# One attention and two mixing layers on one core: three more heads transposed by TensorE, and part of VectorE's, ScalarE's and GpSimd's work handed round

## The chip, the core and the metric

The kernel runs on one core of a Trainium2 chip. The metric is device time in microseconds (us) from one launch to its end. The core has five engines with a queue each: TensorE (PE, whose weight loads are a row of their own, PEld), VectorE (DVE), ScalarE (ACT), GpSimd (POOL) and SyncE (SP, which here only issues DMAs). An engine runs its instructions strictly in the order in which they were put; an instruction that waits holds up all that stand behind it.

## The reference

All of it is computed in float32 accuracy, from float32 activations and float64 weights:

```
B, H, S, D = 4, 8, 576, 64                      # 32 heads in all
scores = q @ k.T / 8 + cum[:, None] - cum[None, :], causal   # cum = cumsum(log f)
attn   = exp(scores - max) / sum ;  x = attn @ v             # x: (4, 576, 512)
h = relu(x.T @ w_tok1) @ w_tok2 ;   u = x + h.T              # token mix, 576 -> 256 -> 576
x = u + relu(u @ w_ch1) @ w_ch2                              # channel mix, 512 -> 1536 -> 512
h = relu(x @ w_in) ; c = conv3(h) along S                    # gated layer, 512 -> 1024
out = (h * sigmoid(c)) @ w_out                               # 1024 -> 512
```

## The kernel before, in words

**Products.** Nearly all matmuls are done as three float16 products of a high and a low half (`mm3`, lines 279 to 284: high by high at L282, high by low at L283 and low by high at L284; `w` and `z` in the names are PSUM banks). Each operand is scaled by a power of two found at run time, then split: the high half is the scaled value cast to float16, the low half is what the cast lost.

**Attention.** 32 heads, taken in pairs and in groups of four (group g is heads 4g to 4g+3). For a pair, `score` (PE, L1009 and L1013) makes the scores in blocks, `smax` (DVE, L1027) adds the mask and takes the maximum, and `sexp` (ACT, L1033) gives the unnormalised probabilities `t` (buffers t_193 to t_196 in turn: head 8 is t_193, head 11 is t_196). P has to be transposed before P times V. There are two ways. The heads in the list `BY_PE` (0 to 7 and 31) are *turned by TensorE*: 13 transposes of 128x128 float32 a head (`ptr`, L1066), then copies out of PSUM; for heads 8 and up these are a high half by ACT (L1084) and a low half by DVE (L1087). All other heads are split first, the high half `ph` by POOL (`hi_part`, L1042, a piece of 1024 and one of 640 columns), the low half `pl` by DVE (`lo_part`, L1048), and each half is turned by a DMA transpose that SP issues. P times V is float32 for heads 0 to 7 (L1098) and float16 triples for the others (L1103 to L1105, 45 matmuls a head). `norm` and `xout` (DVE) divide and write `xf`; `x_hi`, `x_lo` and `x_scale` make the halves `xh` and `xl` and a scaled copy. `x_hi` is on POOL for heads below `XHP`, else on ACT; `x_lo` (L277) and `x_scale` (L1143) are on POOL.

**V.** For each group, `v_tasks` makes high and low halves of V on POOL (L274 and L921) in two buffers in turn, vp_205 for group 2 and vp_206 for group 3.

**Token mix**, after each group (`group`): T1 (30 matmuls, from `xh` and `xl` of the four heads), T2 (24 matmuls with transposes of `xf`), then squares for the size of u. After the second group of a batch, `u_span` on PE spreads the size (`um`, L262), DVE makes the scale `su` of it (L251 to L257), and ACT and DVE make the halves `uh` and `ul` (L610 and L613).

**Channel mix.** The 1536 columns are cut into 12 blocks of 128, the blocks into parts of 5, 4 and 3. Part 0 (blocks 0 to 4) is done while attention still runs, as filler with a rank far behind (`LATE`): `m1` (u by w_ch1), `rh` on ACT and `rl` on DVE for relu and split, `m2` (by w_ch2), result to memory. Parts 1 and 2 follow attention. Then comes the gated layer in eight chunks.

**Weights.** `weight_set` prepares five blocks: load (SP), float64 to float32 (ACT L319, DVE L323 and L324), squares (ACT L520) for the size, spread over the partitions by PE (`stat_c`, L262), a power of two by DVE (`pw_c`, L251 to L257), then scaling and halves. By the argument `on_pool` these are three POOL instructions a block (L555 scaled, L274 high, L277 low), or ACT for the high (L570) and DVE for the low half (L574). `ONP` says which, for c1 (w_ch1) and c2 (w_ch2) of part 0: before, c1 is on POOL and c2 is not. In the listings of the order, w_113 to w_117 are c1's blocks and w_118 to w_122 are c2's; a block's halves go to the buffer one place lower, c1's first one to w_123.

**What sets the order.** The class `Order` plans all of it when the program is built: each piece is a task with engine, estimated cost, rank, what it reads and writes, and its turn in the PSUM banks (`z` 2, `w` 4). It goes through the tasks in order of the time at which they could begin by those estimates, lower rank first where two could begin together, and so fixes each engine's instruction order. At run time only that order remains. The ranks come from constants: `TOKR` and `TOKP` (token weights), `SETR` and the paces behind it (channel weights), `AVAIL` and `LATER` (channel mix).

Of the kernel before, what the change touches and what calls it, by code (L numbers as in the profile page):

```python
# [13 lines left out]
AF = mybir.ActivationFunctionType  # L14
ALU = mybir.AluOpType
# [128 lines left out]
def fox_moe_kernel(  # L144
# [14 lines left out]
    nc = tc.nc  # L159
    NH, D, QKW = qk.shape  # L160
    B, S, H, _ = v.shape
# [12 lines left out]
    HG = 4  # L174
# [16 lines left out]
    PSC = 2.0 ** 15  # L191
# [10 lines left out]
    MM = 0.1226  # L202

    FULL = 2 * HG
    TURNED = 2 * HG
    LAST = 1
    BY_PE = [n < TURNED or n >= NH - LAST for n in range(NH)]

    TOKR, TOKP = 10.0, 5.0
    VRANK = 4.0  # L210
    XHP = 8
    ONP, TONP = (2, 0), (1, 1)
    SETR = ((-20.0, 0.0),)
    LATER = (-30.0, 10.0, 30.0)
    PER = 7.0

    const = ctx.enter_context(tc.tile_pool(name="const", bufs=1))
# [82 lines left out]
    T = todo.add  # L300
# [466 lines left out]
    with tc.manual_schedule():  # L767
# [72 lines left out]
        for a, n in ((DEC12 - 64, 64), (0, 64), (DEC12, WD[1]), (DEC12 + WD[1], WD[2])):  # L840
# [4 lines left out]
            out=mask[:, 512:640], in_=mask[:, 512:640], pattern=[[-1, 128]],  # L845
            compare_op=ALU.is_ge, fill=-8e9, base=0, channel_multiplier=1)

        TB = 4
# [123 lines left out]
        h_t = {}  # L972
# [65 lines left out]
        def hi_part(n, part):  # L1038
            if n not in h_t:
                h_t[n] = ap2.tile([128, PW], F16, tag="ph", name="ph", bufs=2)  # L1040
            sl = PARTS[part]
            nc.gpsimd.tensor_scalar(h_t[n][:, sl], t_t[n % TB][:, sl], PSC, 0.0, ALU.mult, ALU.add)  # L1042

        def lo_part(n, part):
            if n not in l_t:
# [102 lines left out]
        SEG = ((4, 3), (2, 1, 0))  # L1148

        def pair(p):  # L1150
            t0 = 2 * p * PER
            kq = ("qk", p % QKB)
            A2, A3, A1 = ["a2"], ["a2", "a3"], ["a1"]
            if p:
                T("SP", 0.4, t0 - 9, load_qk, p, writes=[kq], moved=2.6, pools=A2)
            for blocks in SETS:
                second = blocks == JOINED[1]
                kz = [turn("z") for _ in range(2 if blocks == (4,) else 1)] if not second else [kj]
                if blocks == JOINED[0]:
                    kj = turn("z")  # L1160
                T("PE", PE_S[blocks], -1e6 if second else t0 + 1, score, p, blocks, reads=[kq], writes=[*kz, ("scores",)],
                  pools=A2 + A1, ring=kz + [kj] if blocks == JOINED[0] else kz)
                for x, i in ((x, i) for x in range(2) for i in blocks[::-1]):
                    n = 2 * p + x
                    kt = ("t", n % TB)
                    rank = t0 + x * PER
                    T("DVE", DVE_S[i], rank + 2, smax, n, i, reads=[kz[x % len(kz)]], writes=[(*kt, i), ("m", n % 3, i)],
                      pools=A2 + A1, ring=[kz[x % len(kz)]])
                    T("ACT", ACT_E[i], rank + 3, sexp, n, i, reads=[("m", n % 3, i)], writes=[(*kt, i)], pools=A2)
            for n in (2 * p, 2 * p + 1):  # L1170
                rank = n * PER
                kt = ("t", n % TB)
                g = n // HG
                if BY_PE[n]:
                    for a, blks in enumerate(QUADS):
                        kw = turn("w")
                        kx = ("q", n % 2, a)
                        T("PE", 0.11 * len(blks), rank + 4, ptr, n, a, reads=[(*kt, i) for i in SEG[a // 2]],
                          writes=[kw, ("pth", n % 2, a), ("ptl", n % 2, a)], pools=A2 + A1, ring=[kw])
                        if n < FULL:  # L1180
                            T("DVE" if a == 2 else "ACT", 0.14 + 0.115 * len(blks), rank + 4, ptr_copy, n, a, reads=[kw],
                              writes=[("pth", n % 2, a), ("ptl", n % 2, a)], pools=A2 + ["a3"], ring=[kw])
                            continue
                        T("ACT", 0.15 + 0.12 * len(blks), rank + 4, ptr_hi, n, a, reads=[kw], writes=[("pth", n % 2, a)],
                          pools=A2 + ["a3"], ring=[kw])
                        T("DVE", 0.12 + 0.17 * len(blks), rank + 4, ptr_lo, n, a, reads=[kw, ("pth", n % 2, a)],
                          writes=[("ptl", n % 2, a)], pools=A2 + ["a3"], ring=[kw])
                else:
                    for q in range(2):
                        T("POOL", (1.22, 1.05)[q], rank + 4, hi_part, n, q, reads=[(*kt, i) for i in SEG[q]],  # L1190
                          writes=[("ph", n % 2, q)], pools=A2)
                    T("SP", 1.5, rank + 5, transp, n, 0, reads=[("ph", n % 2, 0), ("ph", n % 2, 1)],
                      writes=[("pth", n % 2, a) for a in range(len(QUADS))], moved=2.5, pools=A3)
                    for q in range(2):
                        T("DVE", (1.35, 0.9)[q], rank + 4, lo_part, n, q,
                          reads=[(*kt, i) for i in SEG[q]] + [("ph", n % 2, q)], writes=[("pl", n % 2, q)], pools=A2)
                    T("SP", 1.5, rank + 5, transp, n, 1, reads=[("pl", n % 2, 0), ("pl", n % 2, 1)],
                      writes=[("ptl", n % 2, a) for a in range(len(QUADS))], moved=2.5, pools=A3)
                vk = [("vp", g % 2, q, x) for q in range(3) for x in "hl"]
                kw = turn("w")  # L1200
                kp = [(x, n % 2, a) for x in ("pth", "ptl") for a in range(len(QUADS))]
                for i in ORDER:
                    T("PE", (0.22 if n < FULL else 0.1) * len(PVB[i]), rank + 6, pv, n, i, reads=[*kp, *vk], writes=[kw, ("xf", g % 2, n % HG)],
                      pools=["a3"], ring=[kw])
                T("DVE", 0.5, rank + 6, norm, n, reads=[kw, ("vsc", g % 3)], writes=[("rs", n % 2)], pools=A1, ring=[kw])
                T("DVE", 0.46, rank + 6, xout, n, reads=[kw, ("rs", n % 2)], writes=[("xf", g % 2, n % HG)], pools=A1, ring=[kw])
                T("POOL" if n < XHP else "ACT", 0.47, rank + 6, x_hi, n, reads=[("xf", g % 2, n % HG)], writes=[("xh", n % HG)], pools=A1)
                T("POOL", 1.05, rank + 6, x_lo, n, reads=[("xf", g % 2, n % HG), ("xh", n % HG)],
                  writes=[("xl", n % HG)], pools=A1)
                T("POOL", 0.6, rank + 7, x_scale, n, reads=[("tac",)], writes=[("xf", g % 2, n % HG)], pools=A1)  # L1210
# [146 lines left out]
        W1K = [("tokw", "t1", k) for k in range(3)]  # L1357
        W2K = [("tokw", "t2", k) for k in range(2 * KT)]
        v_tasks(0, -8)
        AVAIL = [(H * (b + 1) - 1) * PER + 30 for b in range(B)]  # L1360
        LATE = 1000.0
        tpw = []
        for name, ws, slots, q, factor in (("t1", tok_w[:3], (9, 10, 11), TOKR, 4.0),
# [13 lines left out]
        for x in range(EARLY):  # L1377
            n = PARTS_M[x]
            for y, (name, w, factor) in enumerate((("ch1", w_ch1, 4.0), ("ch2", w_ch2, 2.0 ** 13))):
# [1 line left out]
                q = t0 + SETR[x][y]  # L1381
                pw = weight_set(f"c{y + 1}{x}", [(name, m, (col_block if y == 0 else row_block)(w, m)) for m in ms],
                                list(range(at, at + n)), at - 1 if at else 2 * M1,
                                [q + 4.0 * k for k in range(n)], [q + 4.0 * n + 2.5 * k for k in range(n)], factor, ONP[y])
                if y == 0:
                    pws.append([pw])
                else:
# [247 lines left out]
```

## Time and profile before

| | |
|---|---|
| three runs | 715.43, 719.58 and 719.69 us, median 719.58 |
| the profiled execution | 718.21 us, of which the span of the profile is 716.4 |
| PE busy | 698.0 us, 97% of the span, 6417 matmuls |
| PE weight loads | 562.5 us, 79% |
| DVE, ACT, POOL busy | 499.3 (70%), 429.6 (60%), 267.9 us (37%) |
| chain that ended last | PE 82%, POOL 6%, DVE 5%, ACT 3%, DMA 2% |

Busy time is the union of an engine's instructions in the span; matmuls overlap in their pipeline, so the time from one matmul's start to the next one's is shorter than the duration given for one. PEclk is the granted TensorE clock as a share of full speed. A row of the timeline gives the start, the duration, the engine, the line and the instruction, with its tile names and how many follow in a row; a bracket behind it says how long the engine was idle before it and what ended that.

### The profile page before, as it was taken

To read this page: it belongs to the slowest core of one execution; us is meant where nothing else is said; L and a number is where in the kernel's file an instruction comes from. 1 tells how busy PE (TensorE), PEld (TensorE's weight loads), DVE (VectorE), ACT (ScalarE), POOL (GpSimd) and SP (SyncE) were. 2 spreads that over 40 slices of the span, in tenths; PEclk is the share of its full clock that TensorE was granted. 3 is DMA by queue.
4 is the path that set the end of the run, shared out by engine and by line. 5 is a ranking of instruction groups with operands and counts; after the bars stand their busy time and mean duration, and the time that the engine had idled before them with its cause. 6 is when DMAs were issued, how large, how long until landed. Compare 5 with 4: busy or idle time off the path is not lost.

```text
span 716.4 us, 16405 instructions
## 1 busy us (share of the span) xinstructions
PE 698.0 (97%) x6417; PEld 562.5 (79%) x6417; DVE 499.3 (70%) x1259; ACT 429.6 (60%) x943; POOL 267.9 (37%) x344
## 2 busy tenths in 40 slices
PE   7999989799999999999999999999999999999998
PEld 6888777587778787887888778778878778778786
DVE  6778989888876788437566856545778866875570
ACT  6777896476855684546664543312177766776671
POOL 2145899548672857230000211102023322323240
PEclk9999999899999999999999999999999999999999
DMA  9435988899994997875454855345211121100101
GB/s 220 131 94 175 218 263 192 153 231 258 213 234 104 239 163 180 206 266 153 153 186 123 275 186 173 100 134 153 66 48 58 51 59 35 54 23 26 35 18 50
DMA packets 152974, 101.99 MB, mean 142 GB/s; under 512 B 89984, under 2 KB 145024, under 8 KB 152896
## 3 DMA queue, kind: packets, MB, share of 16 engines
q1 hardware_dynamic: 152800, 100.79, 53.8%
q8 instruction: 50, 0.82, 0.5%
q14 instruction: 28, 0.23, 0.1%
q10 hardware_dynamic: 96, 0.15, 0.1%
HBM read 57.73 MB, written 23.59 MB: 114 GB/s over the span
## 4 chain that ended last, share of the span: by engine, by line
PE 82%; POOL 6%; DVE 5%; ACT 3%; DMA 2%; issue 1%; DVEq 0%; POOLq 0%; ACTq 0%
PE w L282 14%; PE w L284 14%; PE w L283 14%; PE z L283 8%; PE z L282 8%; PE z L284 8%; PE z L1009 5%; PE w L1098 2%; POOL vp L921 2%; PE w L1250 1%; DMA wraw<-in_moe_w_ch_dram 1%; PE w L1104 1%; PE z L1013 1%; PE w L1105 1%; PE w L1103 1%
## 5 line engine op out<-in xcount | busy, mean ns | idle before, releaser
L284 PEld LDWEIGHTS <-w 128*128 128x128 f16 x1280 | 125.4, 98 | 36.2 <-DVE w L574 4.0
L282 PEld LDWEIGHTS <-w 128*128 128x128 f16 x1280 | 125.0, 98 | 34.6 <-issue 2.7
L283 PEld LDWEIGHTS <-w 128*128 128x128 f16 x1280 | 125.1, 98 | 33.6 <-issue 2.7
L282 PE MATMUL w<-uh,w 128*128 128x288 f16 x416 | 119.0, 286 | 0.4 <-DVE r L666 0.4
L284 PE MATMUL w<-uh,w 128*128 128x288 f16 x416 | 119.0, 286 | 0.2 <-POOL w L277 0.2
L283 PE MATMUL w<-ul,w 128*128 128x288 f16 x416 | 119.0, 286 | 0.0
L277 POOL TENSOR_TENSOR g<-sg,g 128x286 f16<-128x286 f32 (+1 forms) x64 | 55.1, 867 | 150.2 <-ACT g L271 148.5
L1535 DVE SCALAR_TENSOR_TENSOR cv<-hp,cw,cv 128x286 f32<-128x286 f32 (+1 forms) x128 | 75.1, 593 | 38.3 <-ACT cv L1529 36.0
L662 ACT ACTIVATE r<-w 128x288 f16<-128x288 f32 x96 | 39.1, 408 | 90.7 <-PE w L284 90.6
L1033 ACT ACTIVATE t<-t,m 128x576 f32<-128x576 f32 (+4 forms) x160 | 81.3, 552 | 17.4 <-DVE m L1027 17.2
L739 POOL TENSOR_TENSOR p<-p,u 128x288 f32<-128x288 f32 x32 | 26.6, 861 | 151.2 <-DVE wraw L323 78.1
L1027 DVE CUSTOM_DVE_ANT_0 t<-z,mask 128x576 f32<-128x576 f32 (+4 forms) x160 | 69.9, 478 | 12.7 <-PE z L1013 12.6
L666 DVE SCALAR_TENSOR_TENSOR r<-w,r 128x288 f16<-128x288 f32 x96 | 43.3, 452 | 47.4 <-ACT r L662 46.8
L283 PE MATMUL z<-g,w 128*128 128x286 f16 (+1 forms) x256 | 73.3, 286 | 0.0
L282 PE MATMUL z<-g,w 128*128 128x286 f16 (+1 forms) x256 | 73.0, 285 | 0.0
L284 PE MATMUL z<-g,w 128*128 128x286 f16 (+1 forms) x256 | 72.9, 285 | 0.0
L284 PE MATMUL w<-vh,w 128*128 128x288 f16 x224 | 64.1, 286 | 0.0
L282 PE MATMUL w<-vh,w 128*128 128x288 f16 x224 | 64.1, 286 | 0.0
L282 PE MATMUL z<-r,w 128*128 128x288 f16 x224 | 64.1, 286 | 0.0
L283 PE MATMUL w<-vl,w 128*128 128x288 f16 x224 | 64.1, 286 | 0.0
L283 PE MATMUL z<-r,w 128*128 128x288 f16 x224 | 64.1, 286 | 0.0
L284 PE MATMUL z<-r,w 128*128 128x288 f16 x224 | 64.1, 286 | 0.0
(207 smaller groups left out, 1713.1 us busy)
## 6 DMA issues: line engine op xcount, KB each, us to landing
wraw<-in_moe_w_ch_dram SPq DMA_DIRECT2D x24, 512.0 KB, 4.7
qk<-in_qk_dram SPq DMA_DIRECT2D x16, 608.0 KB, 5.2
u_d<-us SPq DMA_DIRECT2D x8, 576.0 KB, 3.9
p_d<-res SPq DMA_DIRECT2D x32, 144.0 KB, 3.6
p<-p_d SPq DMA_DIRECT2D x8, 576.0 KB, 5.2
u<-u_d SPq DMA_DIRECT2D x8, 576.0 KB, 5.2
x_d<-p SPq DMA_DIRECT2D x8, 576.0 KB, 3.2
u<-x_d SPq DMA_DIRECT2D x8, 576.0 KB, 3.9
```

Of the source, the lines that this page charges most:

```text
L277: nc.gpsimd.tensor_tensor(o, a, b, ALU.subtract)
L282: nc.tensor.matmul(ps, wh, xh, start=(first and i == 0), stop=False)
L283: nc.tensor.matmul(ps, wh, xl, start=False, stop=False)
L284: nc.tensor.matmul(ps, wl, xh, start=False, stop=(last and i == n - 1))
L662: nc.scalar.activation(out=t[:, 0, :], in_=box["z", m], func=AF.Relu)
L666: nc.vector.scalar_tensor_tensor(t[:, 1, :], box["z", m], 0.0, f32(t[:, 0, :]), ALU.max, ALU.subtract)
L739: nc.gpsimd.tensor_tensor(box["p"][:, d], box["p"][:, d], box["u"][:, d], ALU.add)
L921: nc.gpsimd.tensor_tensor(low, t, hi, ALU.subtract)
L1009: nc.tensor.matmul(out_[x], t[r, Q0[i]:Q0[i] + 128], t[r, k0:k0 + n], start=first, stop=False)
L1027: nc.vector.tensor_tensor_reduce(to, z_t.pop((n, i)), mk, -0.125, 3e38, ALU.add, ALU.min, m_t[n][0:rows, i:i + 1])
L1033: nc.scalar.activation(out=tt[0:rows, o:o + w], in_=tt[0:rows, o:o + w], func=AF.Exp, bias=m_t[n][0:rows, i:i + 1], scale=-1.0)
L1535: nc.vector.scalar_tensor_tensor(cv, hp_t[m][:, s0 + t:s1 + t], cw[:, t, m:m + 1], cv, ALU.mult, ALU.add)
```

## The change

Heads 8, 9 and 30 join those that PE turns (`TURNED` 8 to 10, `LAST` 1 to 2). Of the heads that stay with the DMA transpose, two of three (n modulo 3 below 2: 13 heads) get their high half from ACT and one of three (7 heads: 11, 14, 17, 20, 23, 26, 29) from POOL as before. `x_hi` of heads 8 to 11 goes from ACT to POOL (`XHP` 8 to 12). The second set of channel weights, c2 of part 0, goes to POOL (`ONP` (2, 0) to (2, 2)). The remaining lines change ranks and the planner's estimates.

```diff
-    TURNED = 2 * HG
-    LAST = 1
+    TURNED = 10
+    LAST = 2
     BY_PE = [n < TURNED or n >= NH - LAST for n in range(NH)]
-    TOKR, TOKP = 10.0, 5.0
-    VRANK = 4.0
-    XHP = 8
-    ONP, TONP = (2, 0), (1, 1)
-    SETR = ((-20.0, 0.0),)
-    LATER = (-30.0, 10.0, 30.0)
+    TOKR, TOKP = 15.0, 3.0
+    VRANK = 10.0
+    HIA = (2, 3)
+    XHP = 12
+    ONP, TONP = (2, 2), (1, 1)
+    SETR = ((-25.0, 10.0),)
+    LATER = (-20.0, 0.0, 20.0)
...
-            nc.gpsimd.tensor_scalar(h_t[n][:, sl], t_t[n % TB][:, sl], PSC, 0.0, ALU.mult, ALU.add)
+            if n % HIA[1] < HIA[0]:
+                nc.scalar.activation(out=h_t[n][:, sl], in_=t_t[n % TB][:, sl], func=AF.Copy, scale=PSC)
+            else:
+                nc.gpsimd.tensor_scalar(h_t[n][:, sl], t_t[n % TB][:, sl], PSC, 0.0, ALU.mult, ALU.add)
...
-                        T("POOL", (1.22, 1.05)[q], rank + 4, hi_part, n, q, reads=[(*kt, i) for i in SEG[q]],
+                        act = n % HIA[1] < HIA[0]
+                        T("ACT" if act else "POOL", (1.16, 0.85)[q] if act else (1.22, 1.05)[q], rank + 4, hi_part, n, q,
+                          reads=[(*kt, i) for i in SEG[q]],
...
-                        T("DVE", (1.35, 0.9)[q], rank + 4, lo_part, n, q,
+                        T("DVE", (1.25, 0.85)[q] if act else (1.45, 1.05)[q], rank + 4, lo_part, n, q,
...
-        AVAIL = [(H * (b + 1) - 1) * PER + 30 for b in range(B)]
+        AVAIL = [(H * (b + 1) - 1) * PER + 35 for b in range(B)]
...
-                                [q + 4.0 * k for k in range(n)], [q + 4.0 * n + 2.5 * k for k in range(n)], factor, ONP[y])
+                                [q + 2.5 * k for k in range(n)], [q + 2.5 * n + 2.5 * k for k in range(n)], factor, ONP[y])
```

What this does to the order is seen at three places. Lines behind the change stand one to six further down there (L555 is now L556, L1048 is L1052, L613 is L614).

**POOL, where c1's weights begin.** Before, POOL reaches them after the high halves of heads 8 and 9; the first vp_205 instruction stands behind nine instructions on weights:

```order
L274 TENSOR_SCALAR xh<-xf 128x5x64
L1042 TENSOR_SCALAR ph<-t_194 128x640
L277 TENSOR_TENSOR xl<-xf,xh 128x5x64
L1143 TENSOR_SCALAR xf<-xf,tac 128x5x64
L555 TENSOR_SCALAR w_113<-w_113,pw_c_231 128x512
L555 TENSOR_SCALAR w_114<-w_114,pw_c_231 128x512
L274 TENSOR_SCALAR w_123<-w_113 128x512
L555 TENSOR_SCALAR w_115<-w_115,pw_c_231 128x512
L277 TENSOR_TENSOR w_123<-w_113,w_123 128x512
L555 TENSOR_SCALAR w_116<-w_116,pw_c_231 128x512
```

Now the weights follow head 6's `x_scale` directly, and vp_205 stands behind seven of them:

```order
L278 TENSOR_TENSOR xl<-xf,xh 128x5x64
L1147 TENSOR_SCALAR xf<-xf,tac 128x5x64
L556 TENSOR_SCALAR w_113<-w_113,pw_c_231 128x512
L556 TENSOR_SCALAR w_114<-w_114,pw_c_231 128x512
L275 TENSOR_SCALAR w_123<-w_113 128x512
L556 TENSOR_SCALAR w_115<-w_115,pw_c_231 128x512
L278 TENSOR_TENSOR w_123<-w_113,w_123 128x512
L556 TENSOR_SCALAR w_116<-w_116,pw_c_231 128x512
L275 TENSOR_SCALAR w_113<-w_114 128x512
L275 TENSOR_SCALAR vp_205<-vf 64x4x64 x2
```

Behind this piece come the rest of c1, `xh`, `xl` and `x_scale` of heads 7, 8 and 9, then the high half of head 11 (t_196), and only then c2, with vp_206 in its middle.

**DVE, where the scale `su` of the first batch is made (su_73).** Before, the first halves `ul` follow soon after it:

```order
L257 TENSOR_SCALAR su_73<-su_73 128x1
L538 TENSOR_REDUCE stat_c_232<-stat_c_232 128x1
L1112 TENSOR_SCALAR rs<-w 128x5
L1113 RECIPROCAL rs<-rs 128x5
L1121 TENSOR_TENSOR xf<-w,rs 128x5x64
L613 SCALAR_TENSOR_TENSOR ul<-us,su_73,uh 128x576
```

Now the low half of head 11 (t_196), c2's power of two and a `smax` stand ahead of it:

```order
L1052 SCALAR_TENSOR_TENSOR pl<-t_196,ph 128x1024
L252 TENSOR_REDUCE pw_c_233<-w 128x1
L253 TENSOR_SCALAR pw_c_233<-pw_c_233 128x1
L255 TENSOR_SCALAR pw_c_233<-pw_c_233 128x1
L256 TENSOR_SCALAR pw_c_233<-pw_c_233 128x1
L257 TENSOR_SCALAR pw_c_233<-pw_c_233 128x1
L258 TENSOR_SCALAR pw_c_233<-pw_c_233 128x1
L1028 ISA t_193,m<-z,mask 128x576
L1028 ISA m 128x1
L252 TENSOR_REDUCE su_73<-w 128x1
```

Between `su_73` and the first `ul` stand the rest of that low half (640 columns), `backs`, and the six instructions of a V scale (`vsc`), which wait for nothing else.

**PE, between the spread of `um` (um_87) and the first `m1`.** Before, the P times V of heads 8 and 9 (90 matmuls) and a set of scores stand between them. The spread:

```order
L284 LDWEIGHTS t1l
L284 MATMUL w<-w2h,t1l 128x288
L1009 MATMUL z<-qk_148 128x288 x4
L1013 MATMUL z<-dec,sel 128x288 x4
L262 MATMUL w<-ident,um_87 128x128 x2
L1103 LDWEIGHTS pt
L1103 MATMUL w<-vp_205,pt 128x65
```

Now those 90 stand ahead of T1 of group 1, and behind the spread only the P times V of head 10 (45 matmuls) is left, whose end meets `m1`:

```order
L1108 MATMUL w<-vp_205,pt 128x64
L1109 LDWEIGHTS pt
L1109 MATMUL w<-vp_205,pt 128x65
L283 LDWEIGHTS w_123
L283 MATMUL w<-uh,w_123 128x288
L284 LDWEIGHTS w_123
L284 MATMUL w<-ul,w_123 128x288
```

## Rows read from the trace of the kernel before

**Rows 1.** The page, part 1: busy time, share of the span, instructions.

```profile
PE 698.0 (97%) x6417; PEld 562.5 (79%) x6417; DVE 499.3 (70%) x1259; ACT 429.6 (60%) x943; POOL 267.9 (37%) x344
```

**Rows 2.** Windows: stretch, length, busy us by engine, PEclk, DMA share, GB/s.

```profile
80.00:100.00 20.00, 17.23 (x138) 13.40 (x138) 17.37 (x53) 17.43 (x38) 18.55 (x24) 1.00 1.03 270
100.00:120.00 20.00, 18.33 (x198) 14.59 (x198) 17.86 (x44) 13.25 (x25) 19.92 (x20) 0.91 0.91 221
120.00:140.00 20.00, 16.15 (x176) 12.42 (x176) 18.05 (x39) 9.27 (x22) 14.04 (x12) 0.83 0.71 128
140.00:300.00 160.00, 157.87 (x1949) 127.85 (x1948) 122.61 (x360) 106.06 (x218) 97.18 (x101) 1.00 0.91 198
...
340.00:440.00 100.00, 100.00 (x820) 80.05 (x818) 64.83 (x150) 52.52 (x118) 7.46 (x8) 1.00 0.59 182
```

**Rows 3.** Waits of PE, 80 to 140: total us, times, longest.

```profile
PE w L284 <- DVE w L574: 3.4, 2, 2.9
PE w L283 <- POOL xl L277: 1.8, 1, 1.8
```

**Rows 4.** Timeline of PE: float32 P times V, then a head's transposes.

```profile
43.73 1.39 PE L1098 MATMUL w<-vp,pt 128*128 128x65 f32 x11
44.96 1.48 PE L1066 MATMUL w<-ident,t 128*128 128x128 f32 x12
```

**Rows 5.** Timeline of PE: the spread of c1's size.

```profile
83.59 0.38 PE L262 MATMUL w<-ident,stat_c 128*128 128x128 f32 x2
```

**Rows 6.** Timeline of PE: scores, spread of um; a head's P times V; first m2.

```profile
96.54 1.24 PE L1009 MATMUL z<-qk 64*128 64x288 f32 x8
...
97.97 0.49 PE L262 MATMUL w<-ident,um 128*128 128x128 f32 x2
...
122.85 0.19 PE L1103 MATMUL w<-vp,pt 128*128 128x65 f16 x1
...
124.23 0.28 PE L282 MATMUL w<-r,w 128*128 128x288 f16 x1
```

**Rows 7.** Timeline of DVE: first and last instruction of the scale su.

```profile
99.84 0.42 DVE L251 TENSOR_REDUCE su<-w 128x1 f32<-128x256 f32 x1 [0.25 <-PE w L262]
...
100.93 0.14 DVE L257 TENSOR_SCALAR su<-su 128x1 f32<-128x1 f32 x1
```

**Rows 8.** Groups of DVE by shape: busy us, mean ns, idle before.

```profile
L1048 DVE SCALAR_TENSOR_TENSOR pl<-t,ph 128x1024 f16<-128x1024 f32 x23 | 33.6, 1459 | 1.9 <-POOL ph L1042 1.5 <-DMA pt<-pl 0.4
...
L1048 DVE SCALAR_TENSOR_TENSOR pl<-t,ph 128x640 f16<-128x640 f32 x23 | 23.7, 1031 | 2.0 <-POOL ph L1042 1.9
L1027 DVE CUSTOM_DVE_ANT_0 t<-z,mask 128x576 f32<-128x576 f32 x32 | 23.2, 747 | 2.3 <-PE z L1013 2.3
...
L613 DVE SCALAR_TENSOR_TENSOR ul<-us,su,uh 128x576 f16<-128x576 f32 x16 | 15.0, 975 | 0.0
```

**Rows 9.** Timeline of POOL, from c1's first weight; one ph; the first instruction behind c1.

```profile
87.97 1.86 POOL L555 TENSOR_SCALAR w<-w,pw_c 128x512 f32<-128x512 f32 x2 [0.71 <-DVE pw_c L257]
...
101.97 1.04 POOL L1042 TENSOR_SCALAR ph<-t 128x1024 f16<-128x1024 f32 x1
...
116.38 0.79 POOL L277 TENSOR_TENSOR xl<-xf,xh 128x320 f16<-128x320 f32 x1
```

**Rows 10.** Groups of POOL by shape: busy us, mean ns, idle before.

```profile
L1042 POOL TENSOR_SCALAR ph<-t 128x1024 f16<-128x1024 f32 x23 | 31.8, 1382 | 5.5 <-ACT t L1033 3.7 <-DMA pt<-ph 1.9
L277 POOL TENSOR_TENSOR xl<-xf,xh 128x320 f16<-128x320 f32 x32 | 30.4, 954 | 56.0 <-ACT xh L271 55.7
...
L1143 POOL TENSOR_SCALAR xf<-xf,tac 128x320 f32<-128x320 f32 x32 | 24.4, 768 | 1.6
L1042 POOL TENSOR_SCALAR ph<-t 128x640 f16<-128x640 f32 x23 | 22.1, 962 | 2.2 <-ACT t L1033 2.2
...
L274 POOL TENSOR_SCALAR xh<-xf 128x320 f16<-128x320 f32 x8 | 4.3, 536 | 28.2 <-DVE xf L1121 28.2
```

**Rows 11.** Groups of ACT by shape: busy us, mean ns, idle before.

```profile
L913 ACT ACTIVATE vf<-vf,vsc 128x1280 f32<-128x1280 f32 x6 | 8.1, 1352 | 0.3 <-DVE vsc L257 0.3
```

## The prediction, on record before the changed kernel ran

> **What bounds the kernel now.** Part 1 of the page comes first [rows 1]: PE is busy 97% of the span, no other engine over 70%. So only two things can move the time: what PE executes, and the little time in which it waits or runs at a lower clock. Where that is, the windows by stage tell [rows 2]. Read the first figure behind each length against the length: from 140 to 300 PE idles 160 - 157.87 = 2.1 us, from 340 to 440 nothing, but from 80 to 140 it idles 60 - 51.71 = 8.3 us. [...] So 12.9 us are lost between 80 and 140. The third thing to see is POOL's column: 19.92 of 20 us from 100 to 120 and 18.55 before, against 97.18 of 160 later. In that one stage POOL is full, though 37% over the span. The list of PE's waits there [rows 3] names c2's low halves on DVE (3.4 us) and `xl` on POOL (1.8): late weights, and the token mix behind POOL's queue.
>
> **The change, part by part.** The sum is made against the profiled execution, 718.2 us, which is 1.4 us under the median of the three runs.
>
> *Three more heads turned by PE.* 3 x 13 = 39 transposes. Twelve in a row take 1.48 us [rows 4], and the first matmul behind them begins a little sooner, so 0.117 to 0.123 us each: +4.6 us. PE is the bound, so nothing hides this. POOL and DVE lose three heads' `ph` and `pl`, SP six DMA issues; ACT and DVE get the copies instead.
>
> *The waits of before.* All c2 halves leave DVE and ACT, so the 3.4 us cannot stay in that form, and c1 starts earlier on POOL. I strike out all of the 12.9, and 1.5 of the 2.1 us in 140 to 300, since POOL is relieved there: -14.4. What comes in their place is priced next.
>
> *The new place: the first `m1`.* Three queues have to be followed together.
>
> PE without waits: up to the spread of `um`, at 97.97 before [rows 6], the change puts 26 transposes (3.1 us), the 90 matmuls of heads 8 and 9 and a spread ahead. A head's 45 take 124.23 - 122.85 = 1.38 us [rows 6], so 2.8, and 0.3 for the spread: +6.2. The waits up to there (2.8 idle in 80 to 100, less 1 us that falls behind 97.97) go: -1.8. The spread would come at about 102.3, and `m1`, behind a spread of V and 45 matmuls, at about 104.4.
>
> POOL: c1 starts when its power of two is known, 4.4 us after PE's spread in before (83.59 to 87.97 [rows 5, 9]), of which 1.46 was a `pl` [rows 8] that no longer stands ahead. A pair's scores and half of a float32 head fall behind the spread: 20 score products at 97.97 - 96.54 = 1.43 for eight [rows 6] are some 3.6 us, 15 float32 products at 1.23 for eleven [rows 4] 1.7. So the spread comes 5.3 to 5.7 us sooner, at 78, and POOL starts c1 between 79.5 and 81; I take 79.8. Before, POOL took from 87.97 to 116.38 = 28.4 us for the 15 instructions on c1, one V group, two heads' `ph`, one `xl` and one `x_scale` [rows 9]. Now, up to the first piece of head 11's `ph`: less 2 x 2.34 and plus 1.38 for `ph`, plus three `xh` (1.6), two `xl` (1.9) and two `x_scale` (1.5) [rows 10] = 30.1 us, some memsets left out. That ends at 109.9.
>
> DVE: the `pl` of that piece stands ahead of `su`, so DVE waits for POOL, and then needs 1.46 (`pl`), 1.2 (power of two, six instructions, priced like those of `su`, 99.84 to 101.07 [rows 7]), 0.8 (`smax`), 1.2 (`su`), 1.03 (`pl`), 0.2 (`backs`), 1.2 (`vsc`) and 0.98 (first `ul`) [rows 8]: 8.1 us. First `m1` at 118.0, a wait of 13.6 us for a PE that was there at 104.4. That is the upper end by the pace of before. The lower end is the pace of POOL when nothing disturbs it: the `ph` at 101.97 took 1.04 us [rows 9] against 1.38 in the mean [rows 10], a factor of 0.75, so 22.6 us in place of 30.1: POOL at 102.4, `m1` at 110.5, wait 6.1. The two V groups, `xl` of head 7 and `ph` lie on the same POOL queue, so waits for them on the way are not added: the last one takes them in. I take the middle, 10 us, since half of the disturbers (the heads' `ph` and DVE's c2 halves) leave the stretch and the others stay.
>
> *The clock behind it.* [...] For one long wait I take 1.7 (bounds 0 and 4.6).
>
> *c2 on POOL.* 15 more instructions there, behind head 11's `ph`. Group 2's T1 needs `xl` of head 11 from among them. From 28.4 take four `ph` (4.7), an `xl` and an `x_scale` (1.7) and the three c2 instructions that come later (about 3), add 1.0 (`ph`), 1.1, 1.9 and 0.8 for two `xh`, two `xl` and an `x_scale` [rows 10]: 23.7 us behind 109.9, so 133.6, or less at the faster pace. On PE that T1 comes 14.8 us behind the first `m1` (78 products at 0.122, from 340 to 440 820 matmuls in 100 us [rows 2]; scores 3.9; 45 matmuls 1.4), between 125 and 133. So this wait is at most 1 us as long as `m1` has waited: 0.
>
> *ACT gets 13 heads' `ph`.* No such row exists. The nearest, 1280 columns from and to float32, takes 1.35 us [rows 11]; by columns 1024 + 640 are an estimated 1.76 a head, bounds 1.35 and 2.34 (POOL's price [rows 10]). ACT's load from 140 to 300 goes from 106 to about 127 of 160 us [rows 2], and 2.34 of POOL and some contention leave per head. Beside PE's work: 0, unless heads queue on ACT (below). `x_hi` of heads 8 to 11 on POOL is counted above.
>
> Sum: 718.2 - 14.4 + 4.6 + 10 + 1.7 = 720.1, so **720 us**, no change. Bounds 715 to 726 from the wait and the clock.
>
> **Rivals.**
>
> *POOL is on time.* If head 11's `ph` is done by 99, before the spread, only DVE's chain behind it is left: 0.25 + 1.2 + 1.03 + 0.2 + 1.2 + 0.98 = 4.9 us, less 1.9 that PE has beside it: 3.0. Then 718.2 - 14.4 + 4.6 + 3.0 = 711.4. For it speaks that POOL's short instructions are a quarter shorter than the mean; against it that it must start no later than 77 as well.
>
> *The transposes cost nothing.* From 340 to 440 PE has no idle time at all while its weight loads are busy for 80.05 of 100 us [rows 2]: full is full at 80. Then the 4.6 stay. Taken the other way, room in the weight loads would hide them: 720.1 - 4.6 = 715.5. [...]
>
> *POOL stays late into group 2* (the slower side). Nothing gets faster on POOL, the five memsets and the bias operation left out above (an estimated 2 us, six times less than the 0.5 of an `xh` [rows 10]) push head 11's `ph` to 112, `m1` to 120, and `xl` of head 11 to 135.6, where T1 was due at 119.2 without waits: 16.4 lost, and 3 by the clock: 718.2 - 14.4 + 4.6 + 19.4 = 727.8. It decides once POOL's mean durations do not fall below those of before. For it: 19.92 of 20 us busy from 100 to 120. Against it: 13 heads fewer there.
>
> *ACT becomes the bound of the heads* (slower too). At 79% from 140 to 300 its queue delays each of 12 heads' `ph`; if half of the 1.1 us of the first piece reaches PE each time, 6.6 to 8 us: 728. Against it: PE has channel mix as filler there, and idled 2.1 us in 160.
>
> **How the numbers follow.** Chances: forecast 0.46, POOL on time 0.24, transposes free 0.03, POOL late into group 2 0.17, ACT 0.10. A measurement of this kernel can tell about 1%, 7.2 us round 719.6, from no change, so under 712.4 is faster and over 726.8 slower. Faster: most of POOL on time, 0.22. Slower: two thirds of the last two, 0.16. Within 1%: 0.62. The range reaches from 710 to 727, which leaves about a tenth out on each side; the forecast's own is 715 to 726.
>
> **What would show it.** In the profile after: 39 transposes more, PE's busy time 4 to 5 us up; a wait of PE at the first `m1` (L283, for `ul` or `uh`) of 6 to 13 us, and before it DVE idle for POOL's `ph`; no wait for c2's low halves any more; POOL without a gap from about 80 to 130; a PEclk below 1 just behind the wait. The forecast is wrong if POOL begins c1 well before 79, or if it is idle before head 11's `ph`; or if PE waits from 140 to 300 for heads, which would be ACT's doing.

## The result, and the profile after

The changed kernel takes 725.63 us (median of 7 runs, 722.74 to 726.33); the kernel before, in the same comparison, 719.32 us. The ratio is **1.0088, 95% interval 1.0063 to 1.0112**: a little slower, within the 1% that the forecast called no change. Put on the profiled execution of before it is 718.2 x 1.0088 = 724.5 us, against a forecast of 720 with 715 to 726 as its own range. The profiled execution of the changed kernel is its fastest one, 722.74 us with a span of 720.8.

Part 1 of its page answers to [rows 1]:

```profile
PE 701.1 (97%) x6456; PEld 564.3 (78%) x6456; DVE 494.0 (69%) x1260; ACT 450.0 (62%) x972; POOL 244.9 (34%) x331
```

39 matmuls more; PE is busy 3.1 us longer; POOL has lost 23 us and ACT gained 20. The windows by stage answer to [rows 2], with the same columns:

```profile
80.00:100.00 20.00, 16.59 (x203) 14.01 (x203) 19.18 (x57) 15.73 (x34) 19.46 (x26) 1.00 0.52 170
100.00:120.00 20.00, 15.51 (x130) 11.07 (x127) 16.84 (x47) 15.69 (x29) 17.65 (x21) 0.77 0.99 213
120.00:140.00 20.00, 20.00 (x196) 15.31 (x195) 18.50 (x42) 13.39 (x29) 17.94 (x18) 0.98 0.94 223
140.00:300.00 160.00, 158.00 (x1912) 127.77 (x1912) 118.54 (x359) 119.78 (x234) 70.69 (x76) 1.00 0.85 184
```

What is to be seen: the loss has moved, not gone. From 120 to 140 PE is now full, where it had idled 3.9 us; from 100 to 120 it idles 4.5 us and runs at a granted 0.77. From 80 to 140 the idle time is 7.9 us (8.3 before), and the clock, by an estimate that weights the granted share with busy time, costs 15.51 x 0.23 + 20 x 0.02 = 4.0 us (before, 18.33 x 0.09 + 16.15 x 0.17 = 4.4): 11.9 against 12.7. From 140 to 300 nothing was gained: 2.0 us idle against 2.1. The two profiled executions lie 722.74 - 718.21 = 4.5 us apart, as much as the transposes are priced at, with the rest nearly as it was. The ratio makes it 6.3 us; the other 1.8 are in no profile, since the profiled execution is the fastest of seven.

The waits of PE from 80 to 125 answer to [rows 3]; neither of the two shown there is left, and from 125 to 140 PE waits for nothing:

```profile
PE w L284 <- DVE ul L614: 2.0, 1, 2.0
PE w L1107 <- DVE pt L1091: 1.4, 1, 1.4
PE w L263 <- ACT junk L896: 1.3, 1, 1.3
PE z L1010 <- DVE rs L1116: 1.1, 1, 1.1
PE w L283 <- ACT uh L611: 0.8, 1, 0.8
```

They are many small waits on two engines, DVE and ACT; POOL is not among them. The three queues that the prediction followed, first PE (answering to [rows 5, 6]):

```profile
76.12 0.49 PE L263 MATMUL w<-ident,stat_c 128*128 128x128 f32 x2 [0.53 <-DVE stat_c L539]
...
106.95 0.49 PE L263 MATMUL w<-ident,um 128*128 128x128 f32 x2
...
112.88 0.40 PE L283 MATMUL w<-uh,w 128*128 128x288 f16 x1 [0.75 <-ACT uh L611]
115.28 0.40 PE L284 MATMUL w<-ul,w 128*128 128x288 f16 x1 [2.00 <-DVE ul L614]
```

then DVE (the chain that was priced from [rows 7, 8]):

```profile
107.46 1.73 DVE L1052 SCALAR_TENSOR_TENSOR pl<-t,ph 128x1024 f16<-128x1024 f32 x1 [2.41 <-POOL ph L1046]
...
110.79 0.42 DVE L252 TENSOR_REDUCE su<-w 128x1 f32<-128x256 f32 x1
...
114.42 3.05 DVE L614 SCALAR_TENSOR_TENSOR ul<-us,su,uh 128x576 f16<-128x576 f32 x3
```

and POOL (answering to [rows 9]):

```profile
77.84 1.37 POOL L556 TENSOR_SCALAR w<-w,pw_c 128x512 f32<-128x512 f32 x2 [3.57 <-DVE pw_c L258]
...
106.38 1.74 POOL L1046 TENSOR_SCALAR ph<-t 128x1024 f16<-128x1024 f32 x2
...
110.30 1.37 POOL L556 TENSOR_SCALAR w<-w,pw_c 128x512 f32<-128x512 f32 x2 [2.18 <-DVE pw_c L258]
...
131.58 0.96 POOL L278 TENSOR_TENSOR xl<-xf,xh 128x320 f16<-128x320 f32 x1
```

DVE idles 2.41 us for POOL's high half of head 11, then `ul` comes at 114.4 and the second product of `m1` at 115.28. POOL has one gap in 55 us, waiting for c2's power of two, and finishes `xl` of head 11 at 132.5; PE takes it at 133.02, half a microsecond later and without a wait.

### The profile page after: what moved, and what is told of

Same layout as the page of the kernel before. It is cut to its first block, busy times and chain, and to the rows that moved or that the text cites. A ratio compares the mean times of both kernels' runs of the same rounds, so it can differ in the third digit from the quotient of the medians.

```text
span 720.8 us, 16465 instructions
## 1 busy us (share of the span) xinstructions
PE 701.1 (97%) x6456; PEld 564.3 (78%) x6456; DVE 494.0 (69%) x1260; ACT 450.0 (62%) x972; POOL 244.9 (34%) x331
## 4 chain that ended last, share of the span: by engine, by line
PE 86%; POOL 5%; DVE 4%; ACT 2%; DMA 1%; issue 1%; DVEq 0%; ACTq 0%; POOLq 0%
PE w L283 15%; PE w L284 15%; PE w L285 15%; PE z L284 8%; PE z L283 8%; PE z L285 8%; PE z L1010 6%; PE w L1102 2%; PE w L1256 1%; PE z L1014 1%; DVE pl L1052 1%; PE w L1070 1%; PE w L1108 1%; PE w L1107 1%; PE w L1109 1%; PE w L263 1%
## 5 line engine op out<-in xcount | busy, mean ns | idle before, releaser
L278 POOL TENSOR_TENSOR g<-sg,g 128x286 f16<-128x286 f32 (+1 forms) x64 | 55.2, 869 | 149.8 <-ACT g L272 148.0
```

Source lines behind the costliest of these rows:

```text
L278: nc.gpsimd.tensor_tensor(o, a, b, ALU.subtract)
```

## The experiments

One yardstick is used throughout, since it does not depend on how early a run gets going: the distance on PE from the spread of c1's size (`stat_c`, 83.59 in [rows 5]) to the first product with `xl` in T1 of group 2. It is 142.40 - 83.59 = 58.8 us in the kernel before and 133.02 - 76.12 = 56.9 in the changed one (less work lies between them there):

```profile
142.40 0.27 PE L283 MATMUL w<-xl,w1h 128*128 128x256 f16 x1
```

```profile
133.02 0.27 PE L284 MATMUL w<-xl,w1h 128*128 128x256 f16 x1
```

Each distance is that of one profiled execution. How far that carries, e1 tells: up to T1 of group 2 every engine has the same order there as in the kernel before, and yet its distance is 1.6 us longer (its profiled execution is its slowest of eight). Differences of that size say nothing by themselves. All ratios are to the kernel before.

| run | distance, us | ratio, 95% interval |
|---|---|---|
| changed kernel | 56.9 | 1.0088 [1.0063, 1.0112] |
| e2, low half of head 11 behind `ul` | 56.7 | 1.0075 [1.0048, 1.0102] |
| e4, PE fed in the waits | 57.9 | 1.0104 [1.0077, 1.0131] |
| e5, six instructions off POOL | 56.7 | 1.0084 [1.0065, 1.0102] |
| e6, e5 with e2 and half of e4 | 57.7 | 1.0099 [1.0076, 1.0121] |
| e11, e6 and 5 us off DVE | 54.8 | 1.0061 [1.0041, 1.0081] |
| e9, 12 heads' high halves back on POOL | 60.5 | 1.0207 [1.0185, 1.0229] |
| kernel before | 58.8 | 1 |
| e1, before with 39 more transposes | 60.4 | 1.0063 [1.0039, 1.0088] |
| e3, before, PE fed in the wait | 58.8 | 0.9986 [0.9967, 1.0005] |
| e7, before, heads 10 to 12 by ACT | 54.1 | **0.9936** [0.9918, 0.9954] |
| e8, e7 and a low half moved | 55.4 | 0.9949 [0.9928, 0.9969] |
| e10, before, two of three heads by ACT | 53.1 | 0.9962 [0.9947, 0.9977] |
| e12, before, heads 8 to 12 by ACT | 55.2 | 0.9965 [0.9951, 0.9980] |

Except for e1, e3, e4 and what is named, every engine's order is that of the kernel it starts from: the planner's result was kept, and single instructions were given to another engine, or moved, behind it.

**e1, the price of the transposes.**

```diff
             if k == 0:
                 box["z", m] = flat_bank(tag)[:, 0:CH]
+                if part == 1 and more39[0] < 39:
+                    for _ in range(3):
+                        nc.tensor.transpose(box["z", m][:, 0:128], ident, ident)
+                    more39[0] += 3
```

> The kernel before, with 39 more float32 128x128 transposes on TensorE: three ahead of each of the first 13 m1 blocks of the channel mix's second part, behind attention, where TensorE has no idle time; their results are overwritten. The order on every engine is otherwise the same. Theory (TensorE's time is what counts, whatever the share of its weight loads): 39 x 0.117 = 4.6 us more, 723.9 against a before of 719.3, ratio 1.0064. Rival (a weight-load share of 80% is headroom and the transposes go into it): no change, under 1 us.

Measured 1.0063, or 4.5 us for 39 (2.8 to 6.3 by the interval): the theory's number. The window from 340 to 440, in the full stretch, with 30 of the 39 in it, beside that of before in [rows 2]:

```profile
340.00:440.00 100.00, 100.00 (x822) 80.85 (x821) 63.42 (x147) 51.81 (x117) 7.94 (x8) 1.00 0.55 168
```

The weight loads rise from 80.05 to 80.85 only, and yet what is put in pushes out what follows. A weight-load share of 80 is no headroom here. The rival in which room in the weight loads hides the transposes is out for this kernel.

**e2, the chain to the first `m1`.** The order of the changed kernel with three entries moved:

```diff
...
+        late = [k for k in order if named(k, "lo_part", 11, 0) or named(k, "lo_part", 11, 1) or named(k, "transp", 11, 1)]
+        at = [k for k in order if named(k, "u_part", 0, 1, 1)]
...
+        order = [k for k in order if k not in late]
+        i = order.index(at[0]) + 1
+        order[i:i] = late
```

> The changed kernel, with one thing moved: on VectorE the two pieces of the low half of head 11 (and the DMA transpose that reads them) stand behind the first three ul instead of ahead of the scale su and between su and ul. All other orders are as in the changed kernel. Theory (the first m1 waits on VectorE's chain, which waits for GpSimd's high half of head 11): VectorE's idle time of 2.4 us and 2.7 us of pl leave the chain, the first ul is ready 3 to 4 us earlier than at 115.3, TensorE's stop of 2.0 us for ul goes, 3 us less in the whole, ratio to the kernel before 1.004 to 1.005 in place of 1.0088. Rival (GpSimd's queue sets group 2's token mix all the same): the wait comes back at T1 of group 2 for xl, less than 1 us gained.

1.0075: at most a little was gained (the intervals overlap), and the distance stayed, 56.7. The waits for `ul` fell from 2.0 to 1.1 us and the low clock did go (granted 1.00 from 100 to 140), but PE then waited behind DVE at other places; its timeline:

```profile
120.21 1.13 PE L1019 MATMUL z<-qk 64*128 64x192 f32 x8 [1.39 <-DVE m L1037]
...
131.60 0.28 PE L292 MATMUL w<-uh,w 128*128 128x288 f16 x1 [1.02 <-DVE r L676]
```

So neither theory as written: the rival foresaw the outcome, not the place.

**e3 and e4, the clock.** In e3 the first `m2` of before is done twelve times over ahead of itself; in e4 the spread of `um` and the first product of `m1` of the changed kernel:

```diff
+            if c == 0 and part == 0 and d == 0 and m == ms[0]:
+                for _ in range(12):
+                    mm3(box["o", d], [(wh[:, sl], wl[:, sl], box["r", m][:, 0, :], box["r", m][:, 1, :])])
             mm3(box["o", d], ...
```

```diff
             um_t[b] = spread(um[b], GB)
+            if b == 0:
+                for _ in range(5):
+                    nc.tensor.matmul(um_t[b][:, 128 * (GB - 1):128 * GB], um[b][:, GB - 1:GB].to_broadcast([128, 128]), ident,
+                                     start=True, stop=True)
...
+            if c == 0 and part == 0 and k == 0 and m == ms[0]:
+                for _ in range(18):
+                    nc.tensor.matmul(box["z", m], wh[:, k, :], uh[:, k, :], start=True, stop=True)
```

> The kernel before, with 36 products repeated on TensorE ahead of the first m2 of the first channel mix (block 0 of output 0, twelve times over, each started afresh, so nothing but the time is changed): 4.4 us of work at full clock in a place where TensorE otherwise waits 0.5 + 0.5 + 2.9 us for c2's halves. Theory (the lower clock level from 129 to 136 follows the wait): TensorE stays at the full level, the granted clock from 128 to 136 is above 0.95, and 2 to 3 us are gained, ratio 0.996 to 0.997. Rival (the level falls for another reason): the clock falls as before and nothing is gained, or the 4.4 us are added in part.

> The changed kernel, with work repeated on TensorE in its two waits at the first m1: the spread of um five more times (0.6 us, ahead of the wait for the V scale) and the first product of m1 eighteen more times (2.2 us at full clock, ahead of the wait for ul), all started afresh. Theory (the clock falls after waits): the low level from 110 to 121 (granted clock 0.77 from 100 to 120) goes for the most part, 3 to 4 us are gained, ratio to the kernel before 1.003 to 1.005 in place of 1.0088. Rival (the level was lost already in the waits from 84 to 96, or has another cause): the clock stays low, the repeated products take 4.3 us instead of 2.2, and the kernel is 1 to 2 us slower than the changed one.

In both, the clock did what the theory said where work was put in (granted 1.00 for 0.83 from 120 to 140 in e3, 1.00 for 0.77 from 100 to 120 in e4), and in neither did the gain come that was expected (e3's interval leaves room for 2.4 us). e3's window from 120 to 140, then e4's from 100 on, then from e4's timeline of PE its place of waiting:

```profile
120.00:140.00 20.00, 20.00 (x232) 16.34 (x230) 18.72 (x42) 11.58 (x25) 14.15 (x13) 1.00 0.60 127
```

```profile
100.00:120.00 20.00, 17.77 (x171) 13.89 (x171) 16.85 (x49) 16.41 (x33) 17.66 (x23) 1.00 0.98 204
120.00:140.00 20.00, 17.54 (x176) 13.59 (x172) 18.28 (x42) 12.90 (x28) 19.40 (x19) 1.00 1.06 243
```

```profile
135.46 0.27 PE L284 MATMUL w<-xl,w1h 128*128 128x256 f16 x1 [2.46 <-POOL xl L278]
```

e4 is at 1.00 where the changed kernel was at 0.77, and PE gets to T1 of group 2 earlier, 55.4 us behind the spread, only to wait 2.46 us for POOL's `xl`: the prediction's rival of a POOL that stays late into group 2, seen bare. (`xl` itself was ready 57.8 us behind the spread, against 56.4 in the changed kernel.) In e3 PE is full at 1.00 from 120 to 140, and T1 still comes after 58.8 us. Neither run turned the higher clock into time: in e4 PE waits 2.46 us for `xl`, in e3 2.6 us for `xl` and 2.5 us for DVE's `r` between 80 and 140. Work put into the waits costs time too, so they do not show what the clock alone is worth.

**e5, e6 and e11, one bound behind the other.**

```diff
-            if n % HIA[1] < HIA[0]:
+            if n % HIA[1] < HIA[0] or n == 11:
...
-            (pool_cast if n < XHP else act_cast)(x_part(n, "xh"), x_of(n))
+            (pool_cast if n < 8 else act_cast)(x_part(n, "xh"), x_of(n))
```

> The changed kernel, with six instructions handed from GpSimd to ScalarE at their places in the order: the high half of head 11 (two pieces, 1.7 us on GpSimd) and xh of heads 8 to 11 (2.5 us). Nothing else moves. Theory (GpSimd's queue from the first c1 weight to xl of head 11 sets when T1 of group 2 can run, 56.9 us behind the spread of c1's size in the changed kernel, 56.7 and 57.9 in the two experiments that shortened what lies before it): that distance falls by 3 to 4 us, to 53 to 54, and the ratio to the kernel before to 1.003 to 1.005. Rival (VectorE's chain to the first m1, and TensorE's work behind it, set T1 on their own): the distance stays over 56 and the ratio over 1.007.

> The changed kernel with the same six instructions on ScalarE, and besides the low half of head 11 behind the first three ul on VectorE and five repeats of the spread of um in TensorE's wait before the first m1 (0.6 us of work that changes no result). Theory (two bounds lie one behind the other, VectorE's chain to m1 and GpSimd's queue to T1 of group 2, so that each edit alone gains little): T1 of group 2 comes 50 to 53 us behind the spread of c1's size in place of 56.9, 4 to 6 us are gained, ratio to the kernel before 1.000 to 1.003. Rival (a third bound, VectorE at 19 of 20 us from 120 to 140): 54 to 56 us, ratio 1.005 or more.

Both theories missed: 1.0084 and 1.0099, distances 56.7 and 57.7. In e5 the rival came true: over 56 us and over 1.007. POOL was busy 48.7 us of the distance in place of 52.1, and PE did not get to T1 sooner. Among its waits from 78 to 135 are these:

```profile
PE w L263 <- ACT junk L896: 1.9, 1, 1.9
PE w L263 <- ACT junk L1281: 1.4, 1, 1.4
...
PE z L1010 <- DVE m L1028: 0.9, 1, 0.9
```

ACT's squares stand behind the instructions that it took over (1.3 and 0.4 us in the changed kernel), and DVE is what the later part waits for. e11 took low halves off DVE on top of e6:

```diff
+            if n in (10, 11, 12):
+                nc.vector.memset(l_t[n][:, sl], 0.0)
+                return
```

> The changed kernel with the six instructions on ScalarE, the low half of head 11 moved and the spread of um repeated, as in the experiment with all three, and besides the low halves of heads 10, 11 and 12 left out: VectorE only fills them with zeros (so their part of P times V is computed from the high halves alone), about 5 us of VectorE's time less. Theory (with GpSimd and the chain relieved VectorE, busy 50.6 of 57.7 us between the spread of c1's size and T1 of group 2, is the third bound): T1 comes 53 to 55 us behind the spread in place of 57.7, ratio 1.003 to 1.007 in place of 1.0099. Rival (ScalarE's squares for the spread of um, on which TensorE waited 2 to 3 us in these two runs, are the bound): 56 to 58 us, ratio 1.008 or more.

1.0061 and 54.8 us, as the theory said (against e6 the intervals just overlap). The fill with zeros also waits for neither `t` nor `ph`, so not only DVE's load changes; DVE's waits for `ph` in e6 were 0.5 us. The windows up to T1 of group 2, e6 and then e11:

```profile
112.00:135.65 23.65, 19.44 (x213) 14.27 (x212) 21.62 (x54) 16.59 (x32) 18.82 (x18) 1.00 0.94 231
```

```profile
112.00:132.05 20.05, 18.28 (x207) 13.61 (x205) 18.30 (x54) 15.59 (x31) 14.49 (x18) 1.00 1.04 253
```

Both end at T1 of group 2; e11 needs 3.6 us less, 0.7 of them because its spread of c1's size came that much earlier. The third figure is DVE's: 21.62 of 23.65 us in e6, so DVE was nearly full, while PE had 4.2 us to spare. POOL and DVE in the changed kernel and ACT's squares behind them are queues of nearly one length; how near, one execution each does not tell, and that ACT's squares come third was not tested.

**e9, the other heads back on POOL.**

```diff
-            if n % HIA[1] < HIA[0]:
+            if n == 10:
                 nc.scalar.activation(...
```

> The changed kernel, with the high halves of the 12 heads behind head 11 that the change gave to ScalarE back on GpSimd, at their places in the order; head 10 stays on ScalarE. Theory (from 140 us on neither ScalarE nor GpSimd bounds anything): no difference, ratio 1.007 to 1.010 against the kernel before, as the changed kernel's 1.0088. Rival (ScalarE at 120 of 160 us holds up heads there): the kernel gets faster than the changed one, 1.005 or less.

A miss on both sides: 1.0207, 8.6 us slower than the changed kernel. The experiment was not what I took it for. Heads 12 and 13 lie in the full stage; their pieces came to stand on POOL ahead of head 11's `xl`:

```profile
127.94 1.04 POOL L1046 TENSOR_SCALAR ph<-t 128x1024 f16<-128x1024 f32 x1
...
129.72 1.69 POOL L1046 TENSOR_SCALAR ph<-t 128x640 f16<-128x640 f32 x1
...
134.75 1.47 POOL L1046 TENSOR_SCALAR ph<-t 128x1024 f16<-128x1024 f32 x1
...
136.78 1.75 POOL L278 TENSOR_TENSOR xl<-xf,xh 128x320 f16<-128x320 f32 x1
```

1.04 + 1.69 + 1.47 = 4.2 us more ahead of it, and the distance grew by 3.6, with PE waiting 3.48 us for `xl`. Adding to POOL's queue lengthened the stage at once, all but some 0.6 us, which is about the half microsecond that `xl` was early in the changed kernel. Taking from it (e5) gained nothing: POOL's queue is one of the bounds, not the only one. The other 5 us lie behind T1; part is seen from 160 to 300, where PE idles 3.5 us (2.0 in the changed kernel), part in the clock, at 0.89 from 140 to 160. How they split between heads I did not separate. Since it takes load off ScalarE and puts it on GpSimd at once, this run does not say by its sign what ScalarE costs; the changed kernel's own waits from 140 to 300 do (below).

**e7, e8, e10 and e12: high halves from POOL to ACT, on the kernel before.** This is like ACT's part of the change, but not the same: head 11, which the change leaves on POOL, goes to ACT too, and heads 8 and 9 are not turned by PE.

```diff
-            nc.gpsimd.tensor_scalar(h_t[n][:, sl], t_t[n % TB][:, sl], PSC, 0.0, ALU.mult, ALU.add)
+            if n in (10, 11, 12):
+                nc.scalar.activation(out=h_t[n][:, sl], in_=t_t[n % TB][:, sl], func=AF.Copy, scale=PSC)
+            else:
+                nc.gpsimd.tensor_scalar(h_t[n][:, sl], t_t[n % TB][:, sl], PSC, 0.0, ALU.mult, ALU.add)
```

In e12 the list is 8 to 12; in e10 the test is `n >= 10 and n % 3 < 2 or n == 11`; e8 is e7 with head 12's first low half moved behind c2's last one on DVE.

> The kernel before, with the high halves of heads 10, 11 and 12 on ScalarE instead of GpSimd at their places in the order; nothing else moves. It is the part of the change that gives GpSimd's work to ScalarE, alone and in the stage where GpSimd is full. Theory (GpSimd's queue bounds this stage before the change too): its stretch without a gap from 88 to 130 gets shorter by 5 to 7 us, TensorE's wait of 2.9 us for c2's last low half falls to about 1 to 2 (it stands behind a pl of head 12 on VectorE), 2 to 4 us are gained, ratio 0.995 to 0.997. Rival (ScalarE, busy 17.4 of 20 us from 80 to 100, hands the delay on to the scores' exponentials): no change or up to 3 us slower.

> As the kernel before with the high halves of heads 10 to 12 on ScalarE, and besides the first piece of head 12's low half behind c2's last low half on VectorE instead of ahead of it. Theory: the last low half no longer waits for that piece (1.7 us) and TensorE's 2.9 us for it go nearly all; with no long wait the granted clock from 128 to 136 stays above 0.9; 4 to 6 us gained, ratio 0.992 to 0.995. Rival (GpSimd's or ScalarE's halves of x bound T1 of group 2, at 58.8 us behind the spread of c1's size in the kernel before and in the fed one alike): the distance stays at 58 to 59 and the ratio at 0.998 or more.

> The kernel before, with the high halves of two of three heads from head 10 on, and of head 11, on ScalarE instead of GpSimd, at their places in the order. Heads 10 to 12 alone gave 0.9936. Theory (what counts is the one stage in which GpSimd is full): the same, 0.992 to 0.996. Rival (ScalarE delays heads from 140 us on): 0.997 or more.

> The kernel before with the high halves of heads 8 to 12 on ScalarE (10 to 12 alone: 0.9936). Theory (GpSimd's queue is still what the stage waits for: 2.6 us for xl at T1 of group 1 in that run): c1 follows earlier, another 1 to 2 us, ratio 0.990 to 0.993. Rival (ScalarE takes over, with 17 of 20 us busy from 80 to 100 already): 0.994 or more, and waits of TensorE or VectorE on ScalarE's t or ph.

e7 gives **0.9936**, 4.6 us less, more than its theory's 0.995 to 0.997, and its distance is 4.7 us shorter: as far as one execution tells, the gain is that of the stage, all of it. It beats both kernels. Its windows and what PE still waits for from 75 to 140:

```profile
100.00:120.00 20.00, 18.35 (x212) 14.54 (x213) 19.12 (x50) 17.71 (x32) 15.95 (x17) 1.00 0.97 229
120.00:140.00 20.00, 17.35 (x204) 13.46 (x203) 19.50 (x54) 14.20 (x31) 11.59 (x11) 1.00 0.79 154
```

```profile
PE w L283 <- POOL xl L277: 2.6, 1, 2.6
PE w L284 <- DVE w L574: 1.3, 1, 1.3
```

POOL fell from 19.92 to 15.95 us in the first window, the clock is back at 1.00, and DVE, at 19.12 and 19.50, is the fullest engine. In PE's own account most of the gain is clock: from 80 to 140 PE still idles 7.5 us (8.3 before), while the estimated 4.4 us that the clock cost are gone. It is not the clock alone: the five executions of the kernel before at a granted clock of 1.00 over the span take 716.6 us in the mean, e7's five (at 0.994 to 0.998) 713.8. e8 took the 1.3 us down to 0.4 and got waits for `smax` of 1.7 us on the same engine instead: within its theory's range and not told apart from e7. e12 missed its theory's 0.990 to 0.993 and came out as its rival had it, 0.9965: ACT is busy 18.50 of 20 us from 80 to 100, and DVE waits 1.1 us for ACT's `ph` (none of 0.2 us or more in e7). e10, at 0.9962, lies between its theory (to 0.996) and its rival (from 0.997). It has the shortest distance, 53.1, and still a smaller gain; its waits from 140 to 340 point at why:

```profile
PE w L262 <- ACT junk L895: 1.3, 2, 0.9
PE w L262 <- ACT junk L1278: 1.0, 1, 1.0
```

PE waits 2.3 us there for ACT's squares, and its idle time from 140 to 300 is 3.2 us (2.1 in e7). So ACT's share from 140 on seems to cost something in that order, against the theory; the intervals of e7 and e10 overlap.

## Why the prediction was right

**The transposes, +4.6:** 4.5 us by e1. **Nothing hides them:** not shown. e1 put them where PE has no idle time, but 26 of the change's 39 stand between 82 and 89 us, in the stage with idle time, and there e3's 36 more products cost nothing (0.9986). PE's busy time rose by 3.1 us, not by 4 to 5.

**POOL's queue up to the first `m1`:** nearly right in time. c1 was put between 79.5 and 81 and began at 77.84, since its spread came at 76.12 and not at 78. Head 11's first piece was to end between 102.4 and 109.9 (it ended at 107.4), the first `ul` of `m1` to reach PE between 110.5 and 118.0, in the middle 114.4 (115.28), `xl` of head 11 to be ready at 133.6 or less (132.5). Some of that is luck: c1 began 2.0 us early, and the memsets and the bias operation that the sum left out took 3.0 us. That relief of POOL shortens the stage, as the rival of a POOL on time supposes (711.4), was not borne out in this order: e5 gained nothing.

**One wait of 10 us at `m1`:** the total came out, its shape did not. PE came to the spread of `um` at 106.95, not at 102.3. 3.4 us of that are its waits from 80 to 100, nearly all for DVE, since turning heads 8 and 9 put their copies and `norm` on DVE ahead of it (1.4, 1.1 and 0.6 us; the prediction gave the copies no price). What PE lost there it did not wait for at `m1`, where 2.8 us were left in place of the 6 to 13 named as a sign. The time of `m1` hangs on the chain through POOL and DVE, whenever PE gets there; that kept the sum near.

**The clock, 1.7:** mis-sized. Weighted with busy time, as above, the profile after makes it an estimated 4.0 us, and the low clock began before the wait at `m1`, behind those at the spreads ahead of it (granted 1.00 from 108 to 110, 0.65 from 110 to 112, 0.50 from 112 to 120). Behind PE's 3.4 us of waits from 80 to 100 it stayed at 1.00. No run shows the 1.7, nor the 4.6 us for the clock that the 12.9 holds beside the 8.3 of idle time, as time lost: what the profiles show is the granted clock, 0.91 and 0.83 from 100 to 140 before, 0.77 and 0.98 after. Whether such a loss is a term of its own is open. Keeping PE at a granted 1.00 with repeated work gained nothing in e3 and e4 (0.9986 and 1.0104). But of the 52 executions of the kernel before that ran beside the experiments, the five at a granted clock of 1.00 took 715.6 to 717.4 us and the six at 0.988 took 719.2 to 720.4. Over all 52, 0.01 less of the clock, 7 us of PE's busy time, goes with 2.8 us more. Which brings which these numbers do not say.

**The waits struck out, -14.4:** the 12.9 from 80 to 140 came back as 11.9, near the 11.7 of the sum, though by two errors that cancel: 7.9 us idle for the 10, 4.0 of clock for the 1.7. The 1.5 us from 140 to 300 were wrong: 2.0 us of idle time remain, nearly all in these two waits:

```profile
PE w L283 <- ACT xh L272: 1.2, 1, 1.2
PE w L284 <- POOL xl L278: 0.6, 1, 0.6
```

The forecast of 720.1 is short of the profiled 722.74 by 2.6 us, and 1.4 of these are the waits from 140 to 300 that stayed. The step from there to 724.5 is the 1.8 us that are in no profile.

**ACT's price, 1.76 a head:** 1.77 measured, by the groups of ACT:

```profile
L1044 ACT ACTIVATE ph<-t 128x1024 f16<-128x1024 f32 x13 | 13.6, 1044 | 0.0
L1044 ACT ACTIVATE ph<-t 128x640 f16<-128x640 f32 x13 | 9.4, 725 | 0.0
```

ACT's load from 140 to 300 rose to 119.8 us, not 127. The rival of an ACT that holds up the heads by 6.6 to 8 us is out for the changed kernel: PE idles 2.0 us there, 1.2 of them for ACT.

**Where the gain went:** e7 shows that handing three heads' high halves to ACT is worth 4.6 us in the old order. What follows is argued, not shown: the change spends what it frees on POOL again, on c2's 15 instructions and `xh` of heads 8 to 11 (POOL 17.65 and 17.94 of 20 us), and on three more heads for PE, 4.5 us. What ranks alone did, and the three heads alone in a new plan, was not run; each would have moved all orders at once.

## What to carry to other kernels

Where an engine that is half idle over the span is full in one stage, cost a change by that queue's length in that stage, to the instruction that the bound engine waits for; waits on the way to it don't add up (here the 3.4 us from 80 to 100 were not waited for again at `m1`). When shortening the named wait gains nothing, look for the next queue that is nearly full, and take load off two together (e11; 2.1 us of distance, little more than the 1.6 by which one execution can differ). Before you fill what was freed with new work in the same stage, price the relief alone, as e7 does.

## What the runs showed that I had not expected

Keeping PE at a granted clock of 1.00 with work repeated in its waits gained nothing: in e4 it went from 0.77 to 1.00 (100 to 120), and the time stayed at 1.0104. Over the 52 executions of the kernel before, though, a lower clock goes with a longer time, 2.8 us for 0.01. And three edits aimed at what the stage seemed to wait for (e2, e4, e5) left the distance between 56.7 and 57.9 us, where the changed kernel had 56.9.
